# A second Strassen level in product 4 of the output matmul, its quarters placed behind h

## The chip, the core and the metric

The kernel runs on one core of one Trainium2 chip. The metric is device time in microseconds, the median of several executions; before the change it is 921.05 us.

## What is computed

A linear attention without softmax, followed by a two-layer block with a leaky relu:

```python
kv = np.einsum('bhsd,bhse->bhde', k, v)
out = np.einsum('bhsd,bhde->bhse', q, kv)
rms = np.sqrt(np.mean(out * out, axis=-1, keepdims=True) + 1e-06)
x = out / rms * g_norm          # then (B,H,S,D) -> (B*S, H*D)
h = x @ w_in
g = np.maximum(0.01 * h, h)
y = g @ w_out
```

There are 8 batches of 8 heads with 576 rows of 64, so x is 4608 x 512; `w_in` is 512 x 2048 and `w_out` 2048 x 512. Everything is fp32. Nearly all of the arithmetic lies in the two last products.

## The kernel before, in words

**Blocks, chunks, slots.** The 4608 rows are nine blocks of 512. Block 0 (`first_block`, L1038) uses plain matmuls. In blocks 1 to 8 the 2048 hidden features are four chunks (`c` = 0 to 3), and a chunk has seven slots (`t` = 0 to 6). A chunk of a block has a running number `n` = 4(i - 1) + c, from 0 to 31.

**Two matmuls by Strassen's scheme (Winograd's form).** For a chunk, h is made by seven products (`product_h`, and from block 2 `product_h_two`, L931, where each of the seven is cut by the same scheme once more into seven matmuls of 128 x 128 x 128). One of the seven steps of `product_h_two` runs in each slot: its quarters 1, 6, 7 and 4 go to one PSUM bank, 2, 5 and 3 to another. The banks are `ha` and `hb` in slots 0, 2, 4 and 6, and `hc` and `hd` in the others in between: for a slot the first bank of the pair holds four quarters of 128 columns and the second holds three. ScalarE copies a fresh bank to SBUF (L952), VectorE adds a later one to what is there (L637, the line of the helper `add`). At a chunk's end eight VectorE additions turn the seven sums into g, four ScalarE activations apply the leaky relu (L833, `relu`), and GpSimd forms four sums of g (`sums_of`, L840) as left sides of the output's products.

**The output's products** are `product_o` (L974). They run through `o_queue`, one step per slot by `go_o`, two slots behind the chunk that they belong to, so a chunk's products begin in slot 2 of the next chunk and end in slot 1 of the one after. A product is four matmuls of 128 x 128 x 256. Products 1, 6, 7 and 4 accumulate one after another in one PSUM bank, `oa` or `oc` by the parity of n; 2, 5 and 3 go to the other. After each product VectorE adds the whole bank to an output tile (`os["11"]`, `"12"`, `"22"`, `"21"`); in a block's first chunk a fresh one is copied by ScalarE (L1003). After a block's last chunk a tile is stored by a DMA.

**Product 2 in quarters.** For n = 4 to 29 product 2 is cut by the same scheme again (class `Second`, L906). Its seven quarters use the fourth, free column group of the `hb` or `hd` bank, one per slot, two chunks after the chunk that made g; VectorE adds each quarter to `os["11"]` behind the h additions of that slot. The order of the whole products then is 1, 5, 6, an empty step, 7, 3, 4. The quarters' left sides are made by GpSimd in `inner_g` (L894), their right sides by `inner_w2`.

**Sums of w_out.** The four sums of w_out that the products 5, 6, 7 and 4 need are made once by GpSimd in block 1, written to DRAM, and read back in two loads for every chunk (`sides_w2`, L663), into `t12` and `t34`.

**What sets the order.** `pin` (`keep_in_program_order`) holds an instruction in the order of the program on its engine. From block 2 on it covers all matmuls, all additions by `add`, and the loads. ScalarE's copies and relus are not pinned; the framework's planner places them. In one slot the program's order is: the h matmuls with their reads and the quarter of product 2; the pieces of attention for the next block that this slot has (`FINE_SLOTS`); sums of x for the next block in slots 20, 21 and 22 of a block's 28 (two, one, one); loads; then `go_o`, the step of the output's products. In slot 6 the first two of the additions that make g stand ahead of the step of `product_o`, the others behind it.

Of the kernel before, what the change touches and what calls it, by code (L numbers as in the profile page):

```python
# [9 lines left out]
F32 = mybir.dt.float32  # L10
# [13 lines left out]
def kernel(  # L24
# [36 lines left out]
    nc = tc.nc  # L61
# [11 lines left out]
    U = 2  # L73
# [25 lines left out]
    NW = U * NE * P  # L99
    w1_all = consts.tile([P, 2 * NC * NW], F32, name="w1_all")  # L100
    stage = consts.tile([P, 3 * NW], F32, name="stage")
    pairs = consts.tile([P, 4 * NW], F32, name="pairs")
    g_all = [consts.tile([P, 4 * U * N2], F32, name=f"g_{i}") for i in range(2)]

    def view(t, lo, *shape):
# [79 lines left out]
    zeros = view(g_all[0], 0, NT)  # L185
    nc.vector.memset(zeros[:, :64], 0.0)
    nc.vector.memset(zeros[:, 64:], 0.0)
    ident = consts.tile([P, P], F32, name="ident")

    def make_ident():  # L190
        pin(nc.gpsimd.memset(ident, 1.0))
# [449 lines left out]
    def sides_w1(c):  # L641
# [9 lines left out]
        def more():  # L651
# [5 lines left out]

    w2_dram = [[dram.tile([P, 2, U, N2], F32, name=f"w2_{c}_{i}") for i in range(2)]
               for c in range(NC)]
    t12, t34 = pair(2, 2, U, N2), pair(3, 2, U, N2)  # L660
    writes = []

    def sides_w2(n):  # L663

        c = n % NC
        b11, b12 = w2_sb[0][c][:, :, :N2], w2_sb[0][c][:, :, N2:]
        b21, b22 = w2_sb[1][c][:, :, :N2], w2_sb[1][c][:, :, N2:]

        def sums(i):
            t = (t12, t34)[i]
            if n >= NC:
                pin(nc.sync.dma_start(t, w2_dram[c][i]))
                return
            if i == 0:
                add(nc.gpsimd, t[:, 0], b12, b11, True)
                add(nc.gpsimd, t[:, 1], b22, t[:, 0], True)
            else:
                add(nc.gpsimd, t[:, 0], b22, b12, True)  # L680
                add(nc.gpsimd, t[:, 1], b21, t12[:, 1], True)
            if (n, i) == (NC - 1, 1):
# [55 lines left out]
    def read(to):  # L738
        nonlocal n_read
        while n_read < min(to, len(reads)):  # L740
# [5 lines left out]
    qc = pair(0, 4, 3, P)  # L746
    xt1 = [work.tile([P, 2, N2], F32, tag="xt1", name="xt1"),
           view(w1_all, RING * NG + 24 * P, 2, N2)]
    xt24 = [work.tile([P, 2, 2, N2], F32, tag="xt24", name="xt24"),
            view(w1_all, RING * NG + 16 * P, 2, 2, N2)]  # L750
    xi = view(stage, 0, 3, 7, P)

    def sides_x(i):


        x = xTs.pop(i)
        b11, b12 = x[:, :2, :N2], x[:, :2, N2:]
        b21, b22 = x[:, 2:, :N2], x[:, 2:, N2:]
        home = i % 2 if i > 1 else 0
        t1, t2, t4 = xt1[home], xt24[home][:, 0], xt24[home][:, 1]  # L760
        if i == 1:
            t4 = opool.tile([P, 2, N2], F32, tag="o", name="xt4", bufs=6)
        t3 = b12
        sides = {1: b11, 2: b21, 3: b22, 4: t4, 5: t1, 6: t2, 7: t3}

        def sums():
            for t, a, b in ((t1, b12, b11), (t2, b22, t1), (t3, b22, b12), (t4, b21, t2)):
                add(nc.vector, t, a, b, True)
                yield

        batches, quarters, at = [], {k: {} for k in ORDER}, 0
        upper, lower = (x[:, h:h + 2, :].rearrange("p r (t v n) -> p t r v n", t=2, v=2)
                        for h in (0, 2))
        for js, y in (((1, 7), upper), ((2, 3), lower),
                      ((6, 4), xt24[home].rearrange("p t r (v n) -> p t r v n", v=2)),
                      ((5,), t1.rearrange("p r (v n) -> p r v n", v=2).unsqueeze(1))):
            terms = [y[:, :, r, v, :] for r in range(2) for v in range(2)]
            terms += [xi[:, k, at:at + len(js), :] for k in range(3)]
            batches.append(terms)
            for n, j in enumerate(js):  # L780
                for k, term in zip((1, 7, 2, 3, 5, 6, 4), terms):
                    quarters[k][j] = term[:, n, :]
            at += len(js)

        def inner(kind):
            for y11, y12, y21, y22, t1, t2, t4 in batches:
                if kind == 0:
                    add(nc.gpsimd, t1, y12, y11, True)
# [90 lines left out]

    gi = view(pairs, 12 * P, 4, P)

    def inner_w2(c):
        y = w2_sb[1][c]
# [7 lines left out]

    def inner_g(c, half):  # L894

        g = g_of(c)[3]
        a11, a21, a12, a22 = (g[:, n, :] for n in range(4))
        s1, s2, s3, s4 = (gi[:, n, :] for n in range(4))
        if half == 0:
            add(nc.gpsimd, s1, a21, a22)  # L900
            add(nc.gpsimd, s2, s1, a11, True)
        else:
            add(nc.gpsimd, s3, a11, a21, True)
            add(nc.gpsimd, s4, a12, s2, True)

    class Second:  # L906
# [17 lines left out]
        def done(self, k, bank):  # L924
            v, s = INTO[k]
            to = self.o[:, v, s * P:s * P + P]
            add(nc.vector, to, bank, to)
            if self.n % NC == NC - 1 and k == ORDER[-1]:
                self.finish("11", self.o)

    def product_h_two(i, c, quarters, to, second):  # L931

# [41 lines left out]
    def product_o(n, g_sides, os, finish, second):  # L974

        c = n % NC
        w_sides, _ = sides_w2(n)
        sums = sides_w2(n + 1)[1] if n + 1 < NC * (NB - 1) else lambda i: None
        if c == 0:

            for key in ("12", "22", "11", "21"):
                os[key] = opool.tile([P, 2, N2], F32, tag="o", name=f"o{key}", bufs=6)


        pieces = ((0, slice(0, N2)), (1, slice(0, P)), (1, slice(P, N2))) \
            if n + 1 == NC * (NB - 1) else None
        into = {1: ("11", True), 5: ("22", True), 2: ("11", False), 6: ("12", True),
                3: ("12", False), 7: ("22", False), 4: ("21", True)}

        def done(i, bank):  # L990
            key, fresh = into[i]
            if isinstance(bank, list):
                for at, (end, (part, cols)) in enumerate(zip(bank, pieces)):
                    to = os[key][:, part, cols]
                    add(nc.vector, to, end, to)
                    if i == ORDER[-1]:
                        finish(key, os[key], part, cols, (nc.sync, nc.scalar)[at % 2])
                if i == 7:
                    finish(key, os[key])
                return  # L1000
            to = os[key].rearrange("p u (v n) -> p (u v) n", v=2)
            if c == 0 and fresh:
                nc.scalar.copy(to, bank)  # L1003
            else:
                add(nc.vector, to, bank, to)
            if c == NC - 1 and i in (2, 7, 3, 4):
                finish(key, os[key])

            if i == (6 if second else 5):
                sums(0)  # L1010
            elif i == 4:
                sums(1)


        yield from strassen((("oa", "oc"), ("oc", "oa"))[n % 2], lambda i, part, r: g_sides[i][:, 2 * r + part, :],
                            lambda i, part, r: w_sides[i][:, r, :], done,
                           (1, 5, 6, None, 7, 3, 4) if second else ORDER,
                           pieces=pieces)

    def go(steps, n=None):  # L1020
        while n is None or n > 0:
# [16 lines left out]
    def first_block(between):  # L1038
# [26 lines left out]
                       start=(now[2] == 0), stop=(n == 2 * NC * U))  # L1065
            between(n, 1)
        for t in range(4):
            o = opool.tile([P, DM], F32, tag="o", name="o", bufs=6)
# [38 lines left out]
    for part in range(2):  # L1107
# [4 lines left out]
    FINE_SLOTS = {1: 1, 2: 1, 4: 1, 9: 1, 10: 2, 11: 1, 12: 1, 15: 1, 16: 2, 17: 2, 18: 1, 19: 1,  # L1112
                  23: 1, 24: 1, 25: 1, 26: 1}
    LATE_SLOTS = (3, 4)

    LAG = 2

# [1 line left out]
    HELD = (22, 24, 26)  # L1119
    o_queue, waited = collections.deque(), 0  # L1120

    seconds = {}

    def second_of(n):
        if n in seconds:
# [9 lines left out]
    for i in range(1, NB):  # L1135
# [4 lines left out]
        for c in range(NC):  # L1140
# [3 lines left out]
            for t in range(7):  # L1144
                slot = 7 * c + t
                go(h_steps, 1)
                if not one:

                    if t == 6:
                        go(h_steps, 1)  # L1150
                    if slot in LATE_SLOTS:
                        go(late, 1)
                    for _ in range(FINE_SLOTS.get(slot, 0)):
                        go(a_steps, 1)
                    if i + 1 < NB:
                        if slot == 20:
                            x_sides, new_quarters, sums, inner = sides_x(i + 1)
                        if slot in (20, 21, 22):
                            go(sums, 2 if slot == 20 else 1)
                        if slot == 24:  # L1160
                            inner(0)
                        elif slot == 25:
                            inner(1)
# [3 lines left out]
                if now - 1 in seconds:  # L1167
# [2 lines left out]
                            inner_g((now - 1) % NC, half)  # L1170
                    if t == 5 and now <= 2 * NC:
                        inner_w2((now - 1) % NC)
                if slot == 4 and not one:
                    while writes:
                        pin(nc.sync.dma_start(*writes.pop()))
# [78 lines left out]
```

## Time and profile before

| | |
|---|---|
| median of 3 executions | 921.05 us (918.84 to 922.62) |
| the profiled execution | 917.78 us, span 916.1 us, granted TensorE clock 1.000 |
| DMA | 200.05 MB, mean 218 GB/s |
| VectorE in 493 to 590 us (one block) | 69.34 of 97 us busy |
| ScalarE, GpSimd in the same stretch | 35.23 us, 38.17 us |

The span goes from the first to the last instruction of the profiled execution. PE is TensorE's matmuls and PEld its weight loads; DVE is VectorE, ACT ScalarE, POOL GpSimd, SP SyncE. The names are those of tiles, by their homes: `pairs`, `stage` and `w_all` are large buffers that are cut into views, `gs` holds sums of g, and the bank that the source calls `oa` appears as `o_a`. An fp32 matmul leaves two records, one for each of its two passes. On VectorE and ScalarE the next instruction often starts before the recorded end of the last one, so starts, not durations, give the pace.

### The profile page before, as it was taken

To read this page: it belongs to the slowest core of one execution; us is meant where nothing else is said; L and a number is where in the kernel's file an instruction comes from. 1 tells how busy PE (TensorE), PEld (TensorE's weight loads), DVE (VectorE), ACT (ScalarE), POOL (GpSimd) and SP (SyncE) were. 2 spreads that over 40 slices of the span, in tenths; PEclk is the share of its full clock that TensorE was granted. 3 is DMA by queue.
4 is the path that set the end of the run, shared out by engine and by line. 5 is a ranking of instruction groups with operands and counts; after the bars stand their busy time and mean duration, and the time that the engine had idled before them with its cause. 6 is when DMAs were issued, how large, how long until landed. Compare 5 with 4: busy or idle time off the path is not lost.

```text
span 916.1 us, 18037 instructions
## 1 busy us (share of the span) xinstructions
PE 909.3 (99%) x6980; PEld 776.3 (85%) x6980; DVE 631.6 (69%) x1168; ACT 328.2 (36%) x645; POOL 370.2 (40%) x438
## 2 busy tenths in 40 slices
PE   9999999999999999999999999999999999999998
PEld 5444448888998999899999999999999999999997
DVE  4876995587457876587756786678659755755565
ACT  5454533242135233533343324332343333223330
POOL 2000355967633473226421642264226422642222
DMA  8999926885599778776886789658765676667632
GB/s 269 236 245 249 248 85 191 280 285 167 166 360 289 228 209 268 233 230 214 255 247 230 219 249 272 222 178 212 242 183 176 187 222 198 185 185 223 197 109 92
DMA packets 90228, 200.05 MB, mean 218 GB/s; under 512 B 9888, under 2 KB 42272, under 8 KB 90144
## 3 DMA queue, kind: packets, MB, share of 16 engines
q1 hardware_dynamic: 79680, 187.04, 68.6%
q10 hardware_dynamic: 10016, 10.69, 3.4%
q8 instruction: 55, 0.90, 0.4%
q0 software_dynamic: 448, 1.18, 0.3%
q14 instruction: 29, 0.24, 0.1%
HBM read 172.39 MB, written 26.48 MB: 217 GB/s over the span
## 4 chain that ended last, share of the span: by engine, by line
PE 96%; DMA 2%; DVE 1%; issue 0%; ACT 0%; POOL 0%; SPq 0%; ACTq 0%; DVEq 0%; POOLq 0%
PE o_a L118 19%; PE o_c L118 18%; PE h_ha L118 11%; PE h_hb L118 11%; PE h_hc L118 8%; PE h_hd L118 8%; PE o_acc L118 6%; PE h_ps L118 6%; PE o_ps L118 3%; PE h_a L118 2%; PE h_b L118 1%; PE h_c L118 1%; PE h_d L118 1%; PE kv_ps L118 1%; DMA pairs<-in_v_dram 1%; DMA v_in<-in_v_dram 1%
## 5 line engine op out<-in xcount | busy, mean ns | idle before, releaser
L637 POOL TENSOR_TENSOR gs<-g 128x512 f32<-128x512 f32 x64 | 81.7, 1277 | 253.3 <-ACT g L833 253.3
L833 ACT ACTIVATE g<-g 128x512 f32<-128x512 f32 x124 | 78.2, 631 | 131.9 <-DVE g L637 131.9
L952 ACT COPY w_all<-h_ha 128x512 f32<-128x512 f32 x84 | 48.9, 582 | 173.5 <-PE h_ha L118 167.8
L118 PE MATMUL o_a<-pairs,gs 128*128 128x256 f32 x384 | 91.3, 381 | 0.0
L118 PE MATMUL o_c<-pairs,gs 128*128 128x256 f32 x376 | 89.2, 380 | 0.0
L637 DVE TENSOR_TENSOR o<-h_hb,o 128x128 f32<-128x128 f32 x104 | 29.8, 287 | 83.8 <-ACT pairs L952 83.7
L637 DVE TENSOR_TENSOR o<-o_c,o 128x512 f32<-128x512 f32 (+1 forms) x91 | 61.2, 672 | 23.9 <-PE o_c L118 23.6
L118 PEld LDWEIGHTS o_a<-pairs,gs 128*128 128x128 f32 x384 | 69.8, 190 | 9.2 <-POOL pairs L637 1.2
L118 PEld LDWEIGHTS o_c<-pairs,gs 128*128 128x128 f32 x376 | 68.3, 190 | 7.6
L637 DVE TENSOR_TENSOR o<-o_a,o 128x512 f32<-128x512 f32 x75 | 51.2, 683 | 28.2 <-PE o_a L118 28.1
L637 POOL TENSOR_TENSOR pairs<-w_all 128x512 f32<-128x512 f32 x8 | 11.1, 1384 | 120.6 <-ACT cut L245 102.3
L118 PE MATMUL h_ha<-stage,w_all 128*128 128x128 f32 x448 | 59.6, 276 | 0.0
L118 PEld LDWEIGHTS h_ha<-stage,w_all 128*128 128x128 f32 x448 | 56.6, 192 | 3.0 <-issue 0.7
L118 PE MATMUL h_ps<-xT,w_all 128*128 128x512 f32 (+1 forms) x136 | 58.0, 570 | 0.9 <-DVE w_all L258 0.9
L118 PE MATMUL o_acc<-w,g 128*128 128x512 f32 x128 | 57.8, 595 | 0.0
L637 DVE TENSOR_TENSOR g<-g,pairs 128x512 f32<-128x512 f32 x84 | 55.7, 689 | 1.9
L637 POOL TENSOR_TENSOR pairs<-g 128x128 f32<-128x128 f32 x52 | 23.9, 459 | 75.4 <-PE h_hb L118 46.7
L118 PEld LDWEIGHTS h_ps<-xT,w_all 128*128 128x128 f32 x136 | 25.5, 190 | 30.0 <-issue 26.6
L637 DVE TENSOR_TENSOR w_all<-h_hc,w_all 128x512 f32<-128x512 f32 x56 | 38.3, 684 | 15.9 <-PE h_hc L118 15.8
L118 PEld LDWEIGHTS o_acc<-w,g 128*128 128x128 f32 x128 | 24.0, 190 | 29.8 <-issue 29.4
L637 DVE TENSOR_TENSOR o<-h_hd,o 128x128 f32<-128x128 f32 x78 | 22.1, 283 | 37.8 <-ACT pairs L952 37.7
L118 PE MATMUL h_hb<-stage,w_all 128*128 128x128 f32 x336 | 46.7, 275 | 0.0
(228 smaller groups left out, 2264.6 us busy)
## 6 DMA issues: line engine op xcount, KB each, us to landing
w_all<-w SPq DMA_DIRECT2D x196, 448.0 KB, 4.2
pairs<-w SPq DMA_DIRECT2D x56, 512.0 KB, 4.3
out_dram<-o ACTq DMA_DIRECT2D x35, 256.0 KB, 4.6
v_in<-in_v_dram SPq DMA_DIRECT2D x29, 288.0 KB, 5.7
k_in<-in_k_dram SPq DMA_DIRECT2D x28, 288.0 KB, 5.1
q_in<-in_q_dram SPq DMA_DIRECT2D x56, 144.0 KB, 6.0
q_in<-in_q_dram SPq DMA_DIRECT2D x56, 140.0 KB, 5.8
w<-stage SPq DMA_DIRECT2D x12, 512.0 KB, 4.6
```

The lines of the kernel that those rows point to most:

```text
L118: pin(nc.tensor.matmul(*args, **kw))
L637: ins = eng.tensor_tensor(out_, a, b_, op=ALU.subtract if minus else ALU.add)
L833: nc.scalar.activation(t, t if src is None else src, func=AF.Prelu, alpha=SLOPE)
L952: nc.scalar.copy(q[:, at], bank)
```

## The change

Product 4 of the chunks n = 8 to 28 is cut by the scheme once more, into seven matmuls of 128 x 128 x 128 (class `Fourth`). They run two chunks later, in slots 1 to 4, directly behind the slot's h matmuls: quarters 1, 2 and 5 in slot 1, 6 and 3 in slot 2, 7 in slot 3, 4 in slot 4. All go to the bank of the chunk's products 1, 6 and 7, in three column groups; 6, 7 and 4 accumulate on quarter 1, and 3 on quarter 5. After each step VectorE adds each quarter to a quarter of `os["21"]`; for a block's first chunk ScalarE copies 1, 5, 6 and 4 instead.

The bank's sum of products 1, 6 and 7 was so far read for tile 22 and, with 4 on top, for 21. Now it is kept over a block in a tile of its own, `os["7"]`, and added to 22 and 21 at the block's end (or after n = 28). The whole products' order becomes 1, empty, 6, 5, 7, 3, empty. `inner_g` makes the left sides for products 2 and 4 together, in instructions of twice the width. The right sides of the quarters are made once by `inner_w4` in chunks 4 to 7, written to DRAM and read back for each chunk; the loads for products 7 and 4 are split and moved. The sums of x for the next block come one per slot in slots 20 to 23. Output tiles get four homes, tile 11 two of its own, and the identity matrix shares the home of a sum of x.

```diff
-    pairs = consts.tile([P, 4 * NW], F32, name="pairs")
+    pairs = consts.tile([P, 4 * NW + 4 * P], F32, name="pairs")
...
-    ident = consts.tile([P, P], F32, name="ident")
+    xt24_home = work.tile([P, 2, 2, N2], F32, tag="xt24", name="xt24")
+    ident = xt24_home[:, 0, 0, :P]
...
-    t12, t34 = pair(2, 2, U, N2), pair(3, 2, U, N2)
+    w4_dram = [dram.tile([P, 7, P], F32, name=f"w4_{c}") for c in range(NC)]
+    t12, t34 = pair(2, 2, U, N2), view(pairs, 28 * P, 2, U, N2)
+    f4 = t34[:, 1].rearrange("p u (v n) -> p (u v) n", v=2)
+    f4_more = view(stage, 21 * P, 3, P)
+
+    def four(n):
+        return 2 * NC <= n < NC * (NB - 1) - 3
...
-        def sums(i):
+        def sums(i, row=None):
             t = (t12, t34)[i]
+            if n >= NC and i:
+                if row != 1:
+                    pin(nc.sync.dma_start(t[:, 0], w2_dram[c][i][:, 0]))
+                if row == 0:
+                    return
+                if not four(n):
+                    pin(nc.sync.dma_start(t[:, 1], w2_dram[c][i][:, 1]))
+                    return
+                pin(nc.sync.dma_start(f4, w4_dram[c][:, :4, :]))
+                pin(nc.sync.dma_start(f4_more, w4_dram[c][:, 4:, :]))
+                return
...
-    gi = view(pairs, 12 * P, 4, P)
+    gi_two = pairs[:, 12 * P:].rearrange("p (a n) -> p a n", a=2)
+    gi_four, gi = (gi_two[:, a, :4 * P].rearrange("p (k n) -> p k n", k=4) for a in range(2))
+
+    def inner_w4():
+
+        y11, y12, y21, y22 = (f4[:, k, :] for k in range(4))
+        t1, t3, t2 = (f4_more[:, k, :] for k in range(3))
+        add(nc.gpsimd, t1, y12, y11, True)
+        add(nc.gpsimd, t3, y22, y12, True)
+        add(nc.gpsimd, t2, y22, t1, True)
+        add(nc.gpsimd, y12, y21, t2, True)
...
-        g = g_of(c)[3]
-        a11, a21, a12, a22 = (g[:, n, :] for n in range(4))
-        s1, s2, s3, s4 = (gi[:, n, :] for n in range(4))
+        g = view(g_all[c % 2], 0, 4, 4, P)
+        a11, a21, a12, a22 = (g[:, n, 2:, :] for n in range(4))
+        s1, s2, s3, s4 = (gi_two[:, :, n * P:n * P + P] for n in range(4))
...
+    class Fourth:
+        STEPS = (1, 2, 5), (6, 3), (7,), (4,)
+        COLUMN = {1: 0, 6: 0, 7: 0, 4: 0, 2: 1, 5: 2, 3: 2}
...
+        def step(self, at):
+            if at == 0:
+                self.bank = ps_m.tile([P, 4, P], F32, tag=self.tag, name=f"f_{self.tag}")
+            for k in self.STEPS[at]:
+                matmul(self.bank[:, self.COLUMN[k], :], lhsT=self.left[k], rhs=self.right[k],
+                       start=(k == 1), stop=True, skip_group_check=True)
+            for k in self.STEPS[at]:
+                bank = self.bank[:, self.COLUMN[k], :]
+                v, s = INTO[k]
+                to = self.o_of("21")[:, v, s * P:s * P + P]
+                if self.n % NC == 0 and k in (1, 5, 6, 4):
+                    nc.scalar.copy(to, bank)
+                else:
+                    add(nc.vector, to, bank, to)
+            if at == 3:
+                self.last()
...
+            if fourth and i == 7:
+                key, fresh = "7", True
+            o_of(key)
...
-            if c == NC - 1 and i in (2, 7, 3, 4):
+            if i == 7 and NC <= n:
+                sums(1, 0)
+            if fourth and i == 7:
+                if c == NC - 1 or not four(n + 1):
+                    add(nc.vector, os["22"], os["22"], os["7"])
+                if c == NC - 1:
+                    finish("22", os["22"])
+            elif c == NC - 1 and i in (2, 7, 3, 4):
                 finish(key, os[key])
...
+            elif i == 4 and NC <= n < 2 * NC:
+                inner_w4()
+                later.extend(([3, lambda: (
+                    pin(nc.sync.dma_start(w4_dram[c][:, :4, :], f4)),
+                    pin(nc.sync.dma_start(w4_dram[c][:, 4:, :], f4_more)))],
+                    [4, lambda: sums(1, 1)]))
...
+        def last():
+            sums(1, 1)
+            if c == NC - 1 or not four(n + 1):
+                add(nc.vector, os["21"], os["21"], os["7"])
+            if c == NC - 1:
+                finish("21", os["21"])
...
-                           (1, 5, 6, None, 7, 3, 4) if second else ORDER,
-                           pieces=pieces)
+        order = ORDER
+        if fourth or four(n - 1):
+            order = (1, None, 6, 5, 7, 3, None if fourth else 4)
+        elif second:
+            order = (1, 5, 6, None, 7, 3, 4)
+        if fourth:
+            fourths[n] = Fourth(n, tags[0], o_of, last)
...
+    FOURTH_AT = (1, 2, 3, 4)
...
+                    if t in FOURTH_AT and four((i - 1) * NC + c - 2):
+                        fourths[(i - 1) * NC + c - 2].step(t - FOURTH_AT[0])
...
-                        if slot in (20, 21, 22):
-                            go(sums, 2 if slot == 20 else 1)
+                        if slot in (20, 21, 22, 23):
+                            go(sums, 1)
```

More of the change, by code (lines that the diff above doesn't have):

```diff
@@ L748 @@
            view(w1_all, RING * NG + 24 * P, 2, N2)]
-    xt24 = [work.tile([P, 2, 2, N2], F32, tag="xt24", name="xt24"),
+    xt24 = [xt24_home,
             view(w1_all, RING * NG + 16 * P, 2, 2, N2)]
@@ L761, in sides_x @@
         if i == 1:
-            t4 = opool.tile([P, 2, N2], F32, tag="o", name="xt4", bufs=6)
+            t4 = opool.tile([P, 2, N2], F32, tag="o11", name="xt4", bufs=2)
         t3 = b12
@@ L929, in done, with __init__ @@
                 self.finish("11", self.o)
+    class Fourth:
+        STEPS = (1, 2, 5), (6, 3), (7,), (4,)
+        COLUMN = {1: 0, 6: 0, 7: 0, 4: 0, 2: 1, 5: 2, 3: 2}
+        def __init__(self, n, tag, o_of, last):
+            self.n, self.tag, self.o_of, self.last = n, tag, o_of, last
+            g = g_of(n % NC)[2]
+            self.left = {1: g[:, 0, :], 2: g[:, 2, :], 4: g[:, 3, :],
+                         **{k: gi_four[:, at, :] for at, k in enumerate((5, 6, 7, 3))}}
+            self.right = {**{k: f4[:, at, :] for at, k in enumerate((1, 4, 2, 3))},
+                          **{k: f4_more[:, at, :] for at, k in enumerate((5, 7, 6))}}
+        def step(self, at):
[14 more added lines that the diff above has]
+                self.last()
     def product_h_two(i, c, quarters, to, second):
@@ L977, in product_o, with o_of @@
         w_sides, _ = sides_w2(n)
-        sums = sides_w2(n + 1)[1] if n + 1 < NC * (NB - 1) else lambda i: None
+        sums = sides_w2(n + 1)[1] if n + 1 < NC * (NB - 1) else lambda i, row=None: None
+        fourth = four(n)
+        def o_of(key):
+            if c == 0 and key not in os:
+                home = {"tag": "o11", "bufs": 2} if key == "11" else {"tag": "o", "bufs": 4}
+                os[key] = opool.tile([P, 2, N2], F32, name=f"o{key}", **home)
+            return os[key]
         if c == 0:
-            for key in ("12", "22", "11", "21"):
-                os[key] = opool.tile([P, 2, N2], F32, tag="o", name=f"o{key}", bufs=6)
+            o_of("11")
         pieces = ((0, slice(0, N2)), (1, slice(0, P)), (1, slice(P, N2))) \
@@ L1005, in done @@
                 add(nc.vector, to, bank, to)
-            if c == NC - 1 and i in (2, 7, 3, 4):
+            if i == 7 and NC <= n:
[6 more added lines that the diff above has]
+            elif c == NC - 1 and i in (2, 7, 3, 4):
                 finish(key, os[key])
-            if i == (6 if second else 5):
+            if i == (6 if second else 5) if order[1] is not None else i == 5:
                 sums(0)
-            elif i == 4:
-                sums(1)
-        yield from strassen((("oa", "oc"), ("oc", "oa"))[n % 2], lambda i, part, r: g_sides[i][:, 2 * r + part, :],
-                            lambda i, part, r: w_sides[i][:, r, :], done,
-                           (1, 5, 6, None, 7, 3, 4) if second else ORDER,
-                           pieces=pieces)
+            elif i == 4 and NC <= n < 2 * NC:
[4 more added lines that the diff above has]
+                    [4, lambda: sums(1, 1)]))
+            elif i == 4:
+                sums(1, 1 if NC <= n else None)
+        def last():
[4 more added lines that the diff above has]
+                finish("21", os["21"])
+        tags = (("oa", "oc"), ("oc", "oa"))[n % 2]
+        order = ORDER
[5 more added lines that the diff above has]
+            fourths[n] = Fourth(n, tags[0], o_of, last)
+        yield from strassen(tags, lambda i, part, r: g_sides[i][:, 2 * r + part, :],
+                            lambda i, part, r: w_sides[i][:, r, :], done, order, pieces=pieces)
+    fourths = {}
     def go(steps, n=None):
@@ L1067, in first_block @@
         for t in range(4):
-            o = opool.tile([P, DM], F32, tag="o", name="o", bufs=6)
+            o = opool.tile([P, DM], F32, tag="o", name="o", bufs=4)
             if t % 2:
@@ L1120 @@
     o_queue, waited = collections.deque(), 0
-    seconds = {}
+    seconds, later = {}, []
     def second_of(n):
@@ L1172 @@
                         inner_w2((now - 1) % NC)
+                for job in list(later):
+                    job[0] -= 1
+                    if job[0] == 0:
+                        job[1]()
+                        later.remove(job)
                 if slot == 4 and not one:
```

## The prediction

> **What bounds the kernel now.** I read the busy shares first, then the waits of TensorE's weight loads, then the timelines of the engines around one boundary between two chunks. The first view has one line that matters:
>
> ```profile
> PE 909.3 (99%) x6980; PEld 776.3 (85%) x6980; DVE 631.6 (69%) x1168; ACT 328.2 (36%) x645; POOL 370.2 (40%) x438
> ```
>
> A busy share alone proves little for pipelined matmuls, so the second view is the waits of the weight loads. The only entry there of an `o` bank on an earlier read by VectorE is one wait of 0.3 us:
>
> ```profile
> PEld o_a L118 <- DVE o L637: 0.3, 1, 0.3
> ```
>
> From 250 us on I also subtracted each matmul's start from the next one's: apart from that wait and single gaps of 0.10 us, TensorE never stops. So the kernel is bound by TensorE's work, every matmul saved is worth its full time, and every wait that the change creates costs its full length too. TensorE around the boundary at 543.55 us (start, duration; eight records are four matmuls in two passes):
>
> ```profile
> 545.34 1.89 PE L118 MATMUL o_a<-w,gs 128*128 128x256 f32 x8
> 547.07 0.38 PE L118 MATMUL h_hc<-xT,w_all 128*128 128x128 f32 x2
> ...
> 548.85 1.89 PE L118 MATMUL o_c<-pairs,g 128*128 128x256 f32 x8
> 550.58 1.05 PE L118 MATMUL h_ha<-stage,w_all 128*128 128x128 f32 x8
> ```
>
> Starts give the prices: four matmuls of 256 columns take 550.58 - 548.85 = 1.73 us, eight of 128 columns take 548.85 - 547.07 = 1.78 us, so one is 0.2225 us. VectorE, same place:
>
> ```profile
> 546.10 2.02 DVE L637 TENSOR_TENSOR g<-g,pairs 128x512 f32<-128x512 f32 x3
> 549.19 0.29 DVE L637 TENSOR_TENSOR o<-h_hb,o 128x128 f32<-128x128 f32 x1 [1.06 <-ACT pairs L952]
> 549.40 0.68 DVE L637 TENSOR_TENSOR o<-o_a,o 128x512 f32<-128x512 f32 x1
> 549.99 0.68 DVE L637 TENSOR_TENSOR w_all<-h_hc,w_all 128x512 f32<-128x512 f32 x1
> 550.59 0.55 DVE L637 TENSOR_TENSOR pairs<-h_hd,pairs 128x384 f32<-128x384 f32 x1
> 551.06 0.28 DVE L637 TENSOR_TENSOR o<-h_hd,o 128x128 f32<-128x128 f32 x1
> 551.25 0.68 DVE L637 TENSOR_TENSOR o<-o_c,o 128x512 f32<-128x512 f32 x1
> ```
>
> and ScalarE:
>
> ```profile
> 548.16 0.63 ACT L833 ACTIVATE g<-g 128x512 f32<-128x512 f32 x1 [0.42 <-DVE g L637]
> 548.70 0.46 ACT L952 COPY pairs<-h_hb 128x384 f32<-128x384 f32 x1
> ```
>
> Here is the point. VectorE is free on average, but not here: the sums that make g run until 548.12; ScalarE's last leaky relu waits for them, its copy of the hb bank comes behind that, and VectorE's add on that bank (549.19) waits for the copy. So slot 1's adds, whose matmuls were done before 549, begin at 549.99, and the third starts at 551.06, which is 7.51 after the chunk's first matmul. Call that offset S.
>
> [...] the trace has 0.111 and 0.216, so cutting 256 into 128 costs little. [...] the add at 549.19 starts 0.03 us after ScalarE's copy of the other columns ends, though its own matmul was long done. [...] the trace has 280 to 292 and 680 to 693, but back to back such a small add follows the last after 0.19 to 0.21. [...] The x sums show it: 0.69 alone, 1.28 and 1.14 beside GpSimd.
>
> **The change, part by part.**
>
> *TensorE's work.* Chunks 8 to 28, 21 of them, lose four matmuls of 256 columns and get seven of 128: 1.73 - 7 x 0.2225 = 0.17 us each, 3.6 in all. The one old wait (0.3 and the 0.10 behind it) goes with the x sum that made it: 4.0 us saved.
>
> *The new rhythm and its wait.* Slot 1 loses product 4 and holds h and three quarters, 1, 2 and 5: it is 1.06 us shorter. Slot 2 brings h and then quarters 6 and 3. Counted from the chunk's first matmul: slot 0 takes 3.51; slot 1's h ends at 5.29, its quarters at 5.96; slot 2's h at 7.74. Then quarter 6 adds into the column of quarter 1, and 3 into that of 5. Both need what VectorE read of slot 1's quarters. VectorE's order is the program's: these three adds stand behind slot 1's h adds, so they start at S + 0.19, S + 0.39 and S + 0.59, and the last ends at S + 0.87. What the restart costs is seen at the one old wait:
>
> ```profile
> 789.03 0.68 DVE L637 TENSOR_TENSOR o<-o_a,o 128x512 f32<-128x512 f32 x1
> 789.76 1.38 PEld L118 LDWEIGHTS o_a<-w,g 128*128 128x128 f32 x7 [0.33 <-DVE o L637]
> ```
>
> The add ends at 789.71, TensorE begins at 789.76, and its first pass takes 0.320 for 0.216, as its weights weren't loaded ahead. So 0.05 and 0.10 come on top, and the wait is S + 1.02 - 7.74 = S - 6.72. Queued behind it on TensorE is everything. I take the wait by bank, as the ScalarE copy shows; if only each quarter's own column counts, 3 is the later one, and it is S - 6.94.
>
> *The size of S.* The steps run two chunks later, in chunks 10 to 30. In the 16 of them that aren't the last of a block, the two timelines give S from 7.49 to 8.46, mean 7.74. Two edits shift it and cancel: five chunks get an add of 0.6 (22 and the kept product 7) into the chain, and in five others product 7 is a copy on ScalarE, not an add of 0.6. So 16 x 1.02 = 16.3. Six have quarters 1 and 5 read by ScalarE; a 128-column copy isn't shown, I extrapolate 0.27 from 0.59 and 0.48 at 512 and 384: 0.1 less each, 15.7.
>
> In the five last chunks S is 10.04, because of the x sums:
>
> ```profile
> 592.83 0.68 DVE L637 TENSOR_TENSOR xt<-xT 128x512 f32<-128x512 f32 x1
> 593.55 0.69 DVE L637 TENSOR_TENSOR xt<-xT,xt 128x512 f32<-128x512 f32 x1
> ...
> 599.56 1.28 DVE L637 TENSOR_TENSOR xT<-xT 128x512 f32<-128x512 f32 x1
> ```
>
> Three stand before slot 1's adds now, two will. The chain loses 0.66, and the sum at 599.56 is replaced by one of 0.7 (alone) to 1.1 (beside GpSimd): S between 8.9 and 9.3. I take 9.1: 5 x 2.38 = 11.9. The waits come to 27.6.
>
> *Costed at nothing.* Later steps: 7 follows 6 after product 1 and h (3.5 us); 4 follows 7 after h alone, where VectorE's add on 7 should end some 0.7 before. Product 5 moves to slot 5, which was empty, with its bank read some two microseconds before. GpSimd's inner sums grow from 0.46 to 0.75 us, four a chunk, 24 us in all; it idles 60%, and they lie in slots 4 to 6, ahead of the g sums. The sums for product 4 of w_out: 16 GpSimd adds of 0.46 and eight writes in chunks 6 to 9. Loads: SyncE issues four for two a chunk, 192 KB more, 4 MB of 200 in all; the lower half goes behind product 7, the quarters behind the last step, four slots (13 us) before use, while a `pairs` load lands in 4.3 us; the h weights behind them on SyncE are five slots ahead. The `o` tiles fill four homes with four tiles: the tightest is product 6 in slot 4, some 4 us after its predecessor's store has landed. The identity in xt24 is read long before. If one of these covers fails, TensorE waits for the lateness itself.
>
> *Sum.* 917.8 (the profiled execution: span 916.1 and 1.7 around it) - 4.0 + 27.6 = 941.4, +2.6%. The profiled execution is 0.36% under the median of 921.05, so I add the same share: 944.5.
>
> **Own range of this case.** By column instead of by bank: 16 x 0.80 - 0.6 + 5 x 2.16 = 23.0, net +19, 940. With quarter adds 0.29 apart instead of 0.20 (+0.2 x 21) and S at 9.3: net +29, 950. So 938 to 951.
>
> **Rivals.**
> 1. *ScalarE's copy moves.* The relus and the copies aren't pinned; a planner lays them. If the hb copy stands before the last relu, VectorE's 1.06 us of idleness at 549.19 goes, and S falls by as much. It decides from S = 6.72 down: nothing waits there. With waits by bank the chunks between 7.8 and 8.1 keep 2.7 in all, the last chunks 5 x 1.32: net +5, 926. With waits by column only the last ones are left: 5 x 1.1, net +1.5, 922.5, no slower beyond 0.5%. For it: ScalarE has a hole of 1.4 us before its second relu. Against it: the order is the same in all chunks of the trace, even where two x sums delay the relus by 1.3.
> 2. *More waits.* If also quarter 4 waits for the add on 7, as attention's pieces (transposes of 1.25 us) push VectorE back in the blocks that have them, or the x sum costs more, some 0.5 us in 20 chunks: +10, 955.
> 3. *No wait at all*, the 4.0 saved: 917. It needs quarter adds that overtake the h adds, which the fixed order excludes.
>
> **Chances.** The main case 0.70 (938 to 951), rival 1 0.15 (920 to 938), rival 2 0.11 (951 to 962), rival 3 0.04. A measurement of this kernel can tell about 0.5% from no change, that is 916.4 to 925.7: faster 0.02, same 0.09, slower 0.89. The range for 8 in 10 leaves out rival 3, the lower part of rival 1 and the upper of rival 2: 927 to 955.
>
> **What would show it.** Right: after the three quarters and slot 2's h, TensorE's weight load for an `o` bank waits on VectorE (or ScalarE) in each of 21 chunks, some 1 us in ordinary ones and over 2 in a block's last; no such wait before quarters 7 and 4; TensorE's own work 3.6 us less. Wrong: no idle TensorE there, an hb copy ahead of the last relu, or waits on DMA or GpSimd instead.

## The result, and the profile after

| | before | after |
|---|---|---|
| median (lowest to highest), four executions each | 921.84 us (918.84 to 923.14) | 949.28 us (947.64 to 951.41) |
| profiled execution, its span | 917.78 us, 916.1 us | 950.45 us, 947.6 us |
| granted TensorE clock | 1.000 | 0.995 |

The ratio is 1.0304, with an interval of 1.0268 to 1.034: slower by 3%, at the place that was forecast and inside the range (927 to 955), 4.8 us above the forecast. First the busy shares after.

```profile
PE 916.2 (97%) x7106; PEld 782.4 (83%) x7106; DVE 658.0 (69%) x1282; ACT 334.0 (35%) x669; POOL 404.6 (43%) x454
```

TensorE's share fell from 99% to 97% in a span that grew by 31.5 us: it waits. (Its busy sum doesn't show the saved work: it rose by 6.9 us, with two stretches at a granted clock of 0.50, told of below, in it. The length of a chunk that waits nowhere, below, is the better measure.) The weight loads' waits after:

```profile
PEld f_oc L118 <- DVE o L638: 20.3, 10, 2.6
PEld f_oa L118 <- DVE o L638: 3.6, 5, 0.8
...
PEld f_oa L118 <- ACT o L985: 0.9, 1, 0.9
```

`f_oa` and `f_oc` are the new quarters of product 4. The columns are the total, how often, and the longest. Before, the only line of this kind was 0.3 us once; now it is 24.8 us in 16 longer waits. Four short ones of 0.11, behind ScalarE, stand beside them; in chunk 10, the first, quarter 6 finds its bank read, and it is quarter 5 in slot 1 that starts 0.15 late, just behind the landing of its right side. So 20 of the 21 chunks have the wait that was forecast. Now the boundary of a chunk, one with the extra add (c = 1, first matmul at 557.99), as the prediction showed it for before. TensorE:

```profile
563.29 0.61 PE L118 MATMUL f_oc<-pairs,g 128*128 128x128 f32 x4
...
565.52 0.39 PE L118 MATMUL h_hb<-w,pairs 128*128 128x128 f32 x2
567.21 0.49 PE L118 MATMUL f_oc<-stage,pairs 128*128 128x128 f32 x2 [1.30 <-DVE o L638]
```

VectorE:

```profile
559.14 0.69 DVE L638 TENSOR_TENSOR o<-o,o 128x512 f32<-128x512 f32 x1
...
561.20 2.02 DVE L638 TENSOR_TENSOR g<-g,pairs 128x512 f32<-128x512 f32 x3
564.28 0.29 DVE L638 TENSOR_TENSOR o<-h_hb,o 128x128 f32<-128x128 f32 x1 [1.06 <-ACT pairs L1012]
...
566.15 0.28 DVE L638 TENSOR_TENSOR o<-h_hd,o 128x128 f32<-128x128 f32 x1
566.35 0.80 DVE L638 TENSOR_TENSOR o<-f_oc,o 128x128 f32<-128x128 f32 x3
```

And ScalarE:

```profile
563.25 0.63 ACT L852 ACTIVATE g<-g 128x512 f32<-128x512 f32 x1 [0.36 <-DVE g L638]
563.79 0.46 ACT L1012 COPY pairs<-h_hb 128x384 f32<-128x384 f32 x1
```

The chain is there link by link: the g sums end at 563.22, the last relu follows, the copy of the hb bank behind it ends at 564.25, VectorE's add on that bank starts at 564.28. The third add of slot 1 starts at 566.15, so S = 8.16. The three adds on quarters 1, 2 and 5 (the record `x3`) end at 567.15, and quarter 6, which could have started at 565.74, starts at 567.21.

In a block's last chunk (c = 3, first matmul at 608.28) an x sum stands in the way:

```profile
614.66 1.28 DVE L638 TENSOR_TENSOR xt<-xT,xt 128x512 f32<-128x512 f32 x1
...
617.52 0.28 DVE L638 TENSOR_TENSOR o<-h_hd,o 128x128 f32<-128x128 f32 x1
```

S is 9.24, and TensorE's gap 2.54. Each of the 21 gaps can be taken from TensorE's starts; the first pass after a gap takes 0.10 more (in the chunk at 557.99 quarter 6 takes 0.32 for 0.22, from 567.21 to the next start at 567.53). The predicted column splits the prediction's sum by the kind of chunk, with S of the kernel before and the two edits of 0.6:

| chunk of a block | predicted S, wait | measured S, wait with the 0.10 |
|---|---|---|
| c = 0 (5) | 7.94, 1.22 | 7.38, 0.79 |
| c = 1 (5) | 8.10, 1.38 | 8.16, 1.56 |
| c = 2 (5) | 7.22, 0.50 | 6.84, 0.21 (chunk 10: 0.22, for the load) |
| c = 3 (5) | 9.1, 2.38 | 9.24, 2.64 |
| the last one, chunk 30 | 7.49, 0.77 | 7.82, 1.00 |
| sum | 28.2, less 0.6 for reads by ScalarE: 27.6 | 27.1 |

Of the 31.5 us by which the spans differ, 27.1 are these waits, and 4.0 of TensorE's work are saved. Two terms are not in the sum on record: block 1 begins 5.5 us later (146.3 for 140.8), and TensorE's clock falls to 0.50 in two stretches beside long waits (from 515.6 and from 816.0 us, 3.41 us each), at most 3.4 us together. -4.0 + 27.1 + 5.5 + 3.4 = 32.0.

### The profile page after: what moved, and what is told of

The parts are those of the page before. It is cut to its first block, busy times and chain, and to the rows that moved or that the text cites. A ratio compares the mean times of both kernels' runs of the same rounds, so it can differ in the third digit from the quotient of the medians.

```text
span 947.6 us, 18547 instructions
## 1 busy us (share of the span) xinstructions
PE 916.2 (97%) x7106; PEld 782.4 (83%) x7106; DVE 658.0 (69%) x1282; ACT 334.0 (35%) x669; POOL 404.6 (43%) x454
## 4 chain that ended last, share of the span: by engine, by line
PE 74%; DVE 13%; DMA 8%; ACT 2%; issue 1%; POOL 1%; SPq 0%; ACTq 0%; DVEq 0%; POOLq 0%
PE o_a L118 14%; PE o_c L118 13%; PE h_ha L118 8%; PE h_hb L118 8%; PE h_hc L118 7%; PE h_hd L118 7%; DVE g L638 6%; DVE o L638 4%; PE o_acc L118 3%; PE o_ps L118 3%; PE h_ps L118 3%; PE f_oa L118 2%; DMA pairs<-in_moe_w_in_dram 2%; DMA stage<-in_moe_w_in_dram 2%; PE f_oc L118 1%
## 5 line engine op out<-in xcount | busy, mean ns | idle before, releaser
L638 DVE TENSOR_TENSOR o<-o_c,o 128x512 f32<-128x512 f32 (+1 forms) x81 | 54.5, 673 | 28.0 <-PE o_c L118 27.6
L638 DVE TENSOR_TENSOR o<-o_a,o 128x512 f32<-128x512 f32 x64 | 43.8, 685 | 24.5 <-PE o_a L118 24.4
L638 POOL TENSOR_TENSOR pairs<-g 128x256 f32<-128x256 f32 x52 | 39.9, 767 | 46.5 <-PE h_hd L118 29.6
L118 PEld LDWEIGHTS o_acc<-w,g 128*128 128x128 f32 x128 | 24.3, 193 | 30.1 <-issue 29.5
```

Of the source, the lines that this page charges most:

```text
L118: pin(nc.tensor.matmul(*args, **kw))
L638: ins = eng.tensor_tensor(out_, a, b_, op=ALU.subtract if minus else ALU.add)
```

## The experiments

Theory A, that of the prediction: quarter 6 waits until VectorE has read slot 1's quarters, and these reads are late by the chain g sums, last relu, hb copy, h adds. Theory B: it is something other than that chain (a load, or more work on VectorE as such), so that TensorE waits about as long wherever quarter 6 stands. The short diffs are against the changed kernel, unless said otherwise.

### Quarters 6 and 3 one product later

```diff
-                    if t in FOURTH_AT and four((i - 1) * NC + c - 2):
+                    if t in FOURTH_AT and t != 2 and four((i - 1) * NC + c - 2):
...
+                    if t == 2 and not one and four((i - 1) * NC + c - 2):
+                        fourths[(i - 1) * NC + c - 2].step(1)
```

> Quarters 6 and 3 are issued behind product 1 of slot 2 instead of directly behind h. Theory A (they wait for VectorE's three adds on quarters 1, 2 and 5, which stand in VectorE's queue behind slot 1's h adds): TensorE gets 1.73 us of other work in front, so the waits of the three ordinary kinds of chunk (0.8, 1.6, 0.2 us) go and the last chunks of a block keep 2.6 - 1.7 = 0.9 us, 4.5 in all instead of 27; the time falls by 22 us to about 927. Theory B (VectorE simply has too much to do around the boundary, so the wait only moves): the waits turn up before the h banks of slots 3 and 4 or before quarter 7, and the time stays within 5 us of 949.

Measured: 937.54 us, 1.0187 (1.0144 to 1.023): between the two. In ordinary chunks the wait is gone, 0.2 us at most. In the last chunks it only moved, to quarter 7 in slot 3: 2.56, 2.64, 2.72, 3.12 and 1.15 us, and chunk 10 waits 1.72 for the load of quarter 1's right side; once, in chunk 27, product 1 waits 0.55. VectorE and then TensorE in a last chunk of this kernel:

```profile
516.52 1.56 DVE L373 TENSOR_TENSOR sum<-sum,sq 128x384 f32<-128x384 f32 x2 [0.42 <-ACT sq L369]
518.01 1.21 DVE L638 TENSOR_TENSOR w_all<-xT,w_all 128x512 f32<-128x512 f32 x1
...
519.74 0.60 DVE L638 TENSOR_TENSOR o<-f_oc,o 128x128 f32<-128x128 f32 x2
```

```profile
517.53 0.39 PE L118 MATMUL h_hd<-w,pairs 128*128 128x128 f32 x2
520.39 0.49 PE L118 MATMUL f_oc<-stage,pairs 128*128 128x128 f32 x2 [2.48 <-DVE o L638]
```

The adds on quarters 6 and 3 now stand behind attention's pieces, an x sum and the add on product 1, and only h lies between them and quarter 7. So A holds for the first step, and the slack of the later steps, costed at nothing, exists only while step 1 stands directly behind h.

### Quarters 1, 2 and 5 one slot earlier

```diff
-    FOURTH_AT = (1, 2, 3, 4)
+    FOURTH_AT = (0, 2, 3, 4)
...
-                        fourths[(i - 1) * NC + c - 2].step(t - FOURTH_AT[0])
+                        fourths[(i - 1) * NC + c - 2].step(FOURTH_AT.index(t))
```

> Quarters 1, 2 and 5 move from slot 1 to slot 0, the rest stays. Theory A: VectorE's three adds now stand ahead of slot 1's h adds and end about 1.0 us after slot 0's add on product 2's quarter, 6.0 to 7.2 us after the chunk's start, before quarter 6 is due at 7.74; all waits of quarters 6 and 3 go. In the last chunks the add on product 3 slips to 8.0 to 8.7, and product 1, due at 8.2, waits 0.6 us, 3 us in all. The time falls by 24 us to about 925. Theory B: the adds push slot 1's h adds back by 0.7 us, the waits turn up at the h banks of slot 3, and the time stays above 940.

Measured: 922.47 us, 1.0026 (1.001 to 1.0042). All waits of quarters 6 and 3 are gone. What is left is one wait in chunk 10:

```profile
PE f_oa L118 <- DMA pairs<-w: 4.1, 1, 4.1
```

This is the first load of the quarters' right sides, which in the changed kernel had one slot more. With it goes a stretch of 3.41 us at half clock (at most 1.7 us); one more wait of 0.86 stands in another chunk. The profiled execution was the longest of the twenty (928.93 us), and in it block 1 also began latest, at 147.9 us; how long the load is waited for in the others is not known. VectorE has the same work as in the changed kernel, so B, more work as such, falls.

### The same, but the first chunk's quarters left in slot 1

```diff
+                    made = (i - 1) * NC + c - 2
+                    at = (1, 2, 3, 4) if made == 2 * NC else FOURTH_AT
+                    if t in at and four(made):
+                        fourths[made].step(at.index(t))
```

> Quarters 1, 2 and 5 in slot 0 for n = 9 to 28, in slot 1 for n = 8, whose right sides are still being loaded in slot 0 (4.3 us of wait in the run with slot 0 throughout, and half speed for 3.4 us behind it). Theory A: no wait over 0.3 us is left in chunks 10 to 30 apart from chance, TensorE's 3.6 us are saved, and the time is 0.2 to 0.5% below the kernel before, 916 to 918. Theory B (the added VectorE, GpSimd and DMA work costs something of its own): 921 or more.

Measured: 917.11 us beside 918.29 for the kernel before, 0.9976 (0.9961 to 0.9991): faster than both kernels, by a little. VectorE in a last chunk:

```profile
600.39 0.29 DVE L638 TENSOR_TENSOR o<-h_hb,o 128x128 f32<-128x128 f32 x1 [1.06 <-ACT pairs L1012]
600.60 0.80 DVE L638 TENSOR_TENSOR o<-f_oc,o 128x128 f32<-128x128 f32 x3
```

The 1.06 us of idleness behind the relu and the copy is unchanged, but the three quarter adds now come right behind it, ahead of the x sum (601.32) and of slot 1's h adds (from 602.52). TensorE of a chunk that waits nowhere, here and then in the kernel before (starts of its first matmul and of the next chunk's):

```profile
828.12 0.38 PE L118 MATMUL h_ha<-xT,w_all 128*128 128x128 f32 x2
...
835.65 0.39 PE L118 MATMUL h_hb<-w,pairs 128*128 128x128 f32 x2
835.87 0.39 PE L118 MATMUL f_oc<-stage,pairs 128*128 128x128 f32 x2
...
850.82 0.38 PE L118 MATMUL h_ha<-xT,w_all 128*128 128x128 f32 x2
```

```profile
826.79 0.39 PE L118 MATMUL h_ha<-xT,w_all 128*128 128x128 f32 x2
...
849.66 0.38 PE L118 MATMUL h_ha<-xT,w_all 128*128 128x128 f32 x2
```

Quarter 6 follows slot 2's h at its usual pace. The chunk takes 22.70 us for 22.87: the 0.17 of the second level are there. Of 4.0 us in all, two waits (0.88 and 0.14) take back 1.0, with the 0.10 behind each 1.2, and in five last chunks quarter 1 starts 0.1 late in slot 0. The measured gain is 2.2, between 0.8 and 3.6.

### The sums of x as before

```diff
-                        if slot in (20, 21, 22, 23):
-                            go(sums, 1)
+                        if slot in (20, 21, 22):
+                            go(sums, 2 if slot == 20 else 1)
```

> The change with the sums of x two, one, one in slots 20 to 22 as before. Theory A: in the last chunks of blocks the third add of slot 1 starts 0.7 to 0.8 us later, and since nothing lies in front of quarter 6, TensorE waits that much longer: 3.4 instead of 2.6 us in 5 chunks, 4 us in all, about 953. Theory B: total VectorE work is the same, so the time stays at 949.

Measured: 955.08 us, 1.0391 (1.0351 to 1.0432). S in the last chunks is 9.96. Of the weight loads' waits, one is new:

```profile
PEld h_hb L118 <- DVE o L638: 2.0, 5, 0.4
```

Part of the delay shows as a wait of slot 2's h for its bank, the rest at quarter 6; together 3.36 in a last chunk, S - 6.60. The longer waits also bring more half clock: the missing clock sums to 11.9 us here.

### The new sums of x alone, on the kernel before

```diff
-                        if slot in (20, 21, 22):
-                            go(sums, 2 if slot == 20 else 1)
+                        if slot in (20, 21, 22, 23):
+                            go(sums, 1)
```

This one is against the kernel before.

> The kernel before with only the sums of x one per slot in slots 20 to 23. It has one wait of 0.4 us that they touch: 0 to 0.4 us less, 921.5, the same within what can be measured. If the first block's later start (5 us in the profile of the changed kernel) came from chance, it can turn up here too; if it belongs to the change's other edits, block 1 begins at 141 us here as in the kernel before.

Measured: 918.75 us beside 919.59, 0.9986 (0.9965 to 1.0007): no difference. The old wait at 789 us is gone, S in the last chunks is 9.31. In the changed kernel the same shift is worth 0.72 us of wait in each last chunk (the run above): where x sums stand matters only with the quarters behind them.

### The copy ahead of the last relu (rival 1)

```diff
-        for t in (g11, g12, g22, g21):
+        for t in (g11, g12, g22):
...
+
+        def rest():
+            relu(g21)
+            sums_of(c, to)
+        held.append(rest)
```

The held part is issued behind slot 0's copies.

> The change with a chunk's last leaky relu (and GpSimd's sums of g) issued behind slot 0's copies, so that ScalarE's copy of the hb bank comes ahead of it: the first rival's order. Theory A: VectorE loses the 1.06 us in which it stood idle for that copy, the third add of slot 1 starts as much earlier, and the waits become 0, 0.5, 0 and 1.6 us for c = 0, 1, 2 and 3, some 10.5 in all instead of 27: about 932. Theory B (the wait isn't set by that chain): no change, 949.

Measured: 939.62 us, 1.0202 (1.0162 to 1.0242), 7.6 us more than expected. The copy did change places, but it does not start at once. VectorE and ScalarE of one chunk (c = 2):

```profile
579.81 2.02 DVE L638 TENSOR_TENSOR g<-g,pairs 128x512 f32<-128x512 f32 x3
...
580.87 0.63 ACT L852 ACTIVATE g<-g 128x512 f32<-128x512 f32 x1
581.91 0.48 ACT L1012 COPY pairs<-h_hb 128x384 f32<-128x384 f32 x1 [0.41 <-DVE g L638]
```

ScalarE idles 0.41 and starts the copy 0.08 after the g sums end at 581.83. The copy writes into `pairs`, which these sums read; that this is why, I infer from the names and the profile's releaser. So S falls by 0.46 in c = 1 and 2, not by 1.06. In c = 3 it is 8.17, a fall of 0.6 beyond that; the x sum beside GpSimd took 1.28 above and one alone takes 0.69, so I infer that it no longer meets GpSimd here. In c = 0 it rose to 7.90, as the first two g sums take 1.01 and 1.21 beside GpSimd, for 0.68 each. The wait is again S - 6.60 (c = 0, 1 and 3), 20.4 in all. The chain is A's; rival 1's lever on S was less than half of what it was taken for.

### The extra add moved behind

```diff
-                if c == NC - 1 or not four(n + 1):
-                    add(nc.vector, os["22"], os["22"], os["7"])
-                if c == NC - 1:
-                    finish("22", os["22"])
...
+        def first():
+            if c == NC - 1 or not four(n + 1):
+                add(nc.vector, os["22"], os["22"], os["7"])
+            if c == NC - 1:
+                finish("22", os["22"])
```

`first` runs at the quarters' first step, when the g sums are done.

> The change with the block's last addition of the kept product 7 to tile 22 moved from slot 6 (ahead of the sums that make g) to slot 1 of the next chunk, behind the adds on quarters 1, 2 and 5. Theory A: in the chunks with c = 1 the third add of slot 1 starts 0.6 us earlier, at 7.5 instead of 8.2 after the chunk's start, and the wait there falls from 1.6 to 0.9 us: 3 to 4 us in all with the last one of n = 28, about 946. Theory B: 949, since VectorE's work is the same.

Measured: 945.79 us, 1.0248 (1.0201 to 1.0294). S in c = 1 falls from 8.16 to 7.42 and the gap from 1.46 to 0.72; in chunk 30, which also has such an add, the gap falls from 0.90 to 0.11. That is 4.5 us of waits, for the 3.0 (5 x 0.6) that the prediction gave this add; in the time it is 4.0 beside the changed kernel of the same set (949.75, below).

### Slot 0 with the old sums of x

```diff
+                    made = (i - 1) * NC + c - 2
+                    at = (1, 2, 3, 4) if made == 2 * NC else FOURTH_AT
...
-                        if slot in (20, 21, 22, 23):
-                            go(sums, 1)
+                        if slot in (20, 21, 22):
+                            go(sums, 2 if slot == 20 else 1)
```

These are the edits of the faster kernel and of the old x sums together.

> The run with quarters 1, 2 and 5 in slot 0 from n = 9 on, with the sums of x two, one, one again. Theory A: in the last chunks slot 0's adds end 0.7 us later, at 7.8 instead of 7.1, so quarter 6, due at 7.74, waits 0.2 to 0.3 us in 5 chunks: 1 to 1.5 us in all, some 918.5, hardly to be told from 917.

Measured: 920.68 us, 1.0011 (0.9992 to 1.003), 0.35% behind the faster kernel.

Five waits of 0.72 are left. They were expected at quarter 6 and smaller; they stand at quarter 1 in slot 0. The second x sum delays VectorE's read of product 7, which is in the bank that quarter 1 starts to write:

```profile
595.19 0.69 DVE L638 TENSOR_TENSOR xt<-xT,xt 128x512 f32<-128x512 f32 x1
595.80 0.68 DVE L638 TENSOR_TENSOR o<-o_c,o 128x512 f32<-128x512 f32 x1
```

```profile
596.54 0.71 PE L118 MATMUL f_oc<-pairs,g 128*128 128x128 f32 x4 [0.55 <-DVE o L638]
```

So the first step has no room for an x sum ahead of it either.

### The changed kernel once more

The kernel is unaltered, so this run shows which terms repeat.

> The changed kernel once more, unaltered, for two things that the first profile left open. Waits of quarter 6: 27 us again, since they follow from the order of work. The first block's late start (146.3 against 140.8 us) and the stretches at half speed: if they are chance, they differ here; if they belong to the change, block 1 begins at 146 again.

Measured: 949.75 us, 1.0312 (1.026 to 1.0365). The waits are the same, 27.0 us, but block 1 begins at 141.3. Where that execution lost more is in a view by stretches: start and end, length, then busy time (count) of PE, PEld, DVE, ACT and POOL, the granted clock, DMA share and GB/s.

```profile
508.00:511.00 3.00, 0.63 (x7) 0.44 (x5) 2.97 (x9) 0.83 (x2) 3.00 (x3) 1.00 0.66 213
511.00:514.50 3.50, 3.50 (x60) 2.04 (x64) 2.19 (x4) 0.00 (x0) 0.94 (x1) 0.54 0.04 15
```

TensorE is busy for 0.63 of 3.00 us in the first stretch (the wait, which ends at 511.00), and then works at half clock for 3.4 us. There are four such stretches in this execution.

The balance against the span of the kernel before (916.1), each term read from the trace; the clock column is the sum of the missing share of the granted clock from 330 us on, an upper bound of what it costs:

| kernel | saved | waits | block 1 later | clock, at most | sum | span difference |
|---|---|---|---|---|---|---|
| after | -4.0 | 27.1 | 5.5 | 3.4 | 32.0 | 31.5 |
| after, once more | -4.0 | 27.0 | 0.5 | 6.8 | 30.3 | 29.8 |
| copy ahead of the relu | -4.0 | 20.4 | 4.3 | 0 | 20.7 | 20.6 |
| quarters in slot 0, the first in slot 1 | -4.0 | 1.2 | 3.6 | 0 | 0.8 | 0.9 |

Block 1's start can be left out altogether. From the first matmul of chunk 10 to that of chunk 31 the kernel before takes 498.66 us; the four, in the order of the table, take 26.4, 29.5 and 16.6 us more and 2.1 us less. The columns "saved", "waits" and "clock" give 26.5, 29.8 and 16.4 more and 2.8 less.

## Why the prediction was right

**What bounds the kernel.** Right. Every wait on TensorE came out at its full length (the balance above), and the kernel nearly without waits is faster, by 2.2 of the 4.0 us saved.

**TensorE's work.** Right: 0.17 a chunk, measured as 22.70 against 22.87. The 0.111 and 0.216 us that the prediction names beside it are the pace of one record, that is of one pass, at 128 and 256 columns. A whole matmul of 128 columns takes 0.2225. The sum used these measured starts, so nothing in it changes.

**The wait and its law.** Right in mechanism, a little off in size. Where VectorE alone reads the quarters (c = 0, 1 and 3), the wait is S - 6.60, for S - 6.72, in the changed kernel and in those with the old x sums, the moved copy and the moved add. The term that was off is the pace of the three quarter adds (128 columns, recorded at some 0.28 us each, for some 0.68 at 512): the second follows the first after 0.31, not 0.20, so the last ends at S + 1.0, not S + 0.87. In the six chunks where ScalarE copies quarters 1 and 5, the copy of 5 is the last read and sets the start: it ends 8.61 after the first matmul of chunk 30, and quarter 6 starts at 8.66. That the wait is by bank and not by column is seen in chunk 19: the add on quarter 1, whose column quarter 6 needs, ended 9.71 after the chunk's first matmul, the one on quarter 5 at 10.24, and quarter 6 started at 10.29. Whether the chip or only the program's own semaphores ask for that, no run separates.

**S.** The sum over the chunks came out (27.1 for 27.6), partly by luck, as errors cancelled. c = 1 and c = 3 were right within 0.14, c = 3 although the x sum taken at 0.7 to 1.1 us took 1.28. c = 0 was taken at 7.94 and is 7.38. ScalarE at the start of such a chunk, in the kernel before (first matmul at 520.69):

```profile
518.80 0.92 ACT L394 COPY spread<-rms 128x384 f32<-128x384 f32 x2
519.63 0.48 ACT L952 COPY pairs<-h_hb 128x384 f32<-128x384 f32 x1
```

and after (first matmul at 534.50):

```profile
530.46 0.93 ACT L395 COPY spread<-rms 128x384 f32<-128x384 f32 x2 [1.79 <-DVE rms L391]
...
532.97 0.48 ACT L1012 COPY pairs<-h_hb 128x384 f32<-128x384 f32 x1 [0.31 <-PE h_hb L118]
```

Before, a copy of attention stood ahead of the copy that starts this chunk's chain; after, it was over earlier, and the chain begins 0.47 sooner. Chunk 30 has a sixth extra add, which the prediction did not count, though the diff shows it (`not four(n + 1)`).

**The two edits that cancel.** The add of 0.6 is confirmed by moving it (0.74 each). The copy for the add on product 7 leaves c = 2 at S = 6.84, 0.98 below the mean of the same chunks before, for the 0.60 named. In chunks 22 and 26, where S was 7.50 before, the fall is 0.66. The rest comes from the earlier blocks and is not this edit's: in chunk 14 the copy that starts the chain comes 1.48 ahead of the first matmul, for 1.01 before, when an activation of attention stood ahead of it.

**Costed at nothing.** TensorE got no wait at quarters 7 and 4 or on an output tile. Two of these covers are thinner than they were told. The later steps' slack is gone as soon as step 1 moves behind product 1. The first load of the quarters' right sides has no slack at all: in chunk 10 quarter 5 waited 0.15 and 0.22 us for it in the two profiles of the changed kernel, and quarter 1, in the same slot, 1.72 in the kernel with quarters 6 and 3 one product later.

**The sum.** 941.4 for the profiled execution came out at 950.45; 944.5 (with 0.36% more than 941.4 it is 944.8) at 949.28. The terms that it has agree to within 0.5 us. What lacked is the half clock beside the long waits: up to 3.4 and 6.8 us in the two profiles. Block 1's start is no part of the change's cost: it lies between 140.8 and 147.9 us in the eleven profiled executions, 146.3 and 141.3 in the two of the changed kernel itself. In the five that begin at 144.4 or later, TensorE waited 1.9 to 5.3 us for a load shortly before 94 us, and half clock went with it (in the changed kernel, after 3.32 us of wait, 0.50 for 3.41 us from 92.4 on); in the six that begin by 142.4 TensorE waits for no load there over 0.8 us, and the clock is full (1.00 in the kernel before). Why these loads land later in some executions stays open.

**Rivals.** 1: tried, and its premise (S falls by 1.06) was wrong, since the copy has a second thing to wait for. 2: no wait at quarter 4; the same mechanism, adds pushed back by attention's pieces, appears at quarter 7 once step 1 is moved. 3: its time of 917 was met by the kernel with the quarters in slot 0. It was ruled out because the quarter adds would have to overtake the h adds; the move puts them ahead of slot 1's h adds in the program's order.

## What to carry to other kernels

Here an accumulation into one bank in consecutive slots tied TensorE to the reader's place in its own queue. So look not at the reader's busy share but at what stands ahead of it at that moment. The remedy was not less work, but one slot of distance between first write and reuse. Before one takes a wait out of a chain, one should look for the second wait that ends just before it. And a cover that holds in steady state must be checked for the first iteration, where loads have not yet run ahead.

## What was not expected of the hardware

TensorE's clock drops to half beside its own waits, well within the stage. Take the waits of 2.5 to 3.1 us from 330 us on in five profiles (the changed kernel twice, quarters 6 and 3 one product later, the old x sums, the moved add): with 17 of 24 goes a stretch of 3.41 us at a granted clock of 0.50, or twice that length (two of them). It begins between 1.0 us before the end of the wait and 1.7 us after it. With the waits of up to 1.7 us in these profiles and in the kernel with the moved copy there was none.

Within each of these profiles, the starts and ends of these stretches lie whole multiples of 3.4133 us apart, to within 0.01 us. In the changed kernel's first profile, for one, stretches begin at 92.38, 515.63 and 816.01 us, which is 124 and 88 such steps. Laid over the 24 waits, this grid sorts them. Where more than 2.0 us of a wait fell into one step of the grid, half clock came in 14 of 14; between 1.7 and 2.0 us in 3 of 6; below in none of 4. What decides in between, and where the grid comes from, stays open. Each stretch of 3.41 us at 0.50 costs at most half its length, 1.7 us, on top of the wait.
